# Loading the last weight matrix of a decode kernel as two tiles, with several DMAs into the second and two rows brought by sixteen 8-partition DMAs

## Chip, cores, metric

The kernel runs on one core of one Trainium2 chip. The metric is the time of one execution on the device in microseconds (us); lower is better. Engine names: PE is the matrix engine, PEld its weight loads, DVE the vector engine, ACT the scalar engine, POOL is GpSimd, SP the engine that issues nearly all DMAs (SPq is its queue of instructions).

## The reference, cut

One token of a gated mix of two blocks. Block A is attention over a long cache (4 key/value heads of 65,536 positions x 128, bf16); block B is a small MLP.

```python
q = x @ wq                                  # 1 x 4096
p = softmax(q @ k.T * Dh ** -0.5); o = p @ v # 32 query heads, 4 kv heads
a = o.reshape(1, 4096) @ wo                 # wo is 4096 x 1024 bf16: 8 MiB
b = (z1 * (w_sp * layernorm(z2) + b_sp)) @ w_out
out = g * a + (1 - g) * b
```

The caches are 134 MB (128 MiB) and everything together 162 MB, read once. The argument below is about the last 8 MiB, `wo`, seen as 32 rows of 256 KB (a row has 2 KB in each of 128 partitions).

## The kernel before

Every load takes one of five 32 KB-per-partition buffers. The output stage, with cuts (`...`):

```python
CT = 128; NKV = 5; OC = 32; D = 1024
WO_SPLIT = (16, 8, 4, 2, 1, 1)
kv = ctx.enter_context(tc.tile_pool(name="kv", bufs=NKV))

def load(src, shape, name):
    t = kv.tile([P, CT * P], BF16, name=name, tag="kv")
    ...
    nc.sync.dma_start(out=v, in_=src)          # L84: all loads are issued here
    return v
...
for j in range(NT):                            # v of the last head: four 4 MiB loads
    rest(v_units(G - 1, j, load_kv(A_v_cache, G - 1, j, "vt")))

def project(src, n, vec, c0, name, first=False, last=False):
    w = load(src, (n, D), name)
    for c in range(n):
        for j in range(NJ):                    # 8 matmuls for a row, L403
            nc.tensor.matmul(out_ps[:, j, :], lhsT=w[:, c, j * P:(j + 1) * P],
                             rhs=vec[:, c0 + c:c0 + c + 1].to_broadcast([P, W]), ...)
...
project(B_w_out..., FC, uT, 0, "wout_t", first=True)
wo_view = A_wo.rearrange("(p c) n -> p c n", c=OC)
c0 = 0
for n in WO_SPLIT:
    project(wo_view[:, c0:c0 + n, :], n, oa, c0, "wo_t", last=(c0 + n == OC))
    c0 += n
out_sb = const.tile([P, NJ], FP32, name="out_sb")
nc.vector.tensor_copy(out=out_sb[:], in_=out_ps[:, :, 0])   # first step of the epilogue
```

The framework that the kernel is written in places all semaphores. In the trace each load increments a semaphore as its data lands (the load of 16 rows 16 times, from 369.2 to 378.2 us).

## Time and profile before

| | before |
|---|---|
| time, median of 3 runs | 392.88 us (392.80 to 393.32) |
| span of the profiled run | 391.5 us |
| HBM read | 162.01 MB, 414 GB/s over the span |
| first matmul on `wo` / copy of the output out of PSUM | 378.24 / 388.66 us |

The page of the profile cuts the span into 40 slices. DMA is the busy share of the 16 DMA engines in tenths, GB/s what they moved:

```profile
DMA  8999999999999999999999999999999999999983
GB/s 329 432 434 435 437 429 433 430 430 425 430 426 430 422 424 415 410 432 434 432 429 430 422 434 432 424 425 435 427 433 434 432 423 429 427 424 428 424 352 119
```

The kernel is bound by bytes until the last two slices. There something else must be asked for: which wait ends last. The chain that ended last, in order of time (start, us, what), ends so:

```profile
344.43 33.77 DMA wo_t<-in_A_wo_dram
378.24 10.39 PE out_ps L403 x256
```

The load of the first 16 rows was issued at 344.43 and landed at 378.2. After it PE runs all 256 matmuls on `wo` without a gap. The busy times of each engine by stretch (from:to, length, busy us and count for each engine, then PE's granted clock, the DMA engines' share, GB/s) show why 256 matmuls take 10.4 us, and that DMA is already half idle at that time:

```profile
375.00:380.00 5.00, 1.76 (x34) 1.76 (x35) 0.00 (x0) 0.00 (x0) 0.00 (x0) 0.68 0.85 359
380.00:385.00 5.00, 5.00 (x116) 5.00 (x114) 0.00 (x0) 0.00 (x0) 0.00 (x0) 0.63 0.48 196
385.00:390.00 5.00, 3.90 (x118) 3.58 (x114) 0.45 (x2) 0.00 (x0) 0.00 (x0) 1.00 0.31 105
```

PE had been idle for 5.8 us before it, and starts at half clock: the granted clock was 0.50 from 376.8 to 383.7 us. Matmuls start 53 ns apart until 383.7, 31 ns apart afterwards. The idle time before a fall of the clock was not the same each time in this trace: at 376.84 PE had been idle for 4.4 us (from 372.44), at 359.77, where the granted clock also fell to half, for 2.0 us only (from 357.79).

Why is DMA half idle from 380 us on? Each load of `wo` increments its semaphore 16 times; they are read here as one increment for each of the 16 DMA engines, when its part of the load is in. The times of the 16 increments, from the semaphore records of the trace (us):

```
16 rows: 369.2 369.2 369.5 369.6 369.9 370.1 370.7 371.2 | 376.1 376.3 376.7 377.7 377.7 377.7 378.0 378.2
1 row:   378.4 378.7 378.8 379.0 379.1 379.3 379.9 380.4 | 385.5 385.8 386.8 386.8 386.8 386.9 387.1 387.3
```

So read, eight engines are about 7 us behind the other eight.

### The profile page before, as it was taken

The numbers are of one execution on the slowest core, as the hardware profiler recorded it, in microseconds if no ns is written. First come the engines' busy times: TensorE is split into PE (matmuls) and PEld (weight loads), VectorE is DVE, ScalarE is ACT, GpSimd is POOL, SyncE is SP. The second block draws the span as 40 slices with busy tenths as digits, with TensorE's granted clock in tenths as the row PEclk, the third lists the DMA queues.
The fourth block names the chain that finished last, engine by engine and source line by source line (L and its number), as shares of the span: only waits on it lengthen the run. The fifth ranks groups of instructions, "written<-read, shape, count | busy, mean of one in ns | idle before, by whom it ended". The sixth has DMA issues, their size and how long they took to land.

```text
span 391.5 us, 14960 instructions
## 1 busy us (share of the span) xinstructions
PE 301.1 (77%) x7080; PEld 291.4 (74%) x7080; DVE 152.3 (39%) x296; ACT 122.4 (31%) x139; POOL 1.0 (0%) x9
## 2 busy tenths in 40 slices
PE   0774379977889789868897878887986877887947
PEld 0774379877878779868897877877885877787836
DVE  2011036656594434435743443465443444300100
ACT  1010025544466233233453323344542323300000
POOL 1000000000000000000000000000000000000000
PEclk9999999999999989999999999999999999998979
DMA  8999999999999999999999999999999999999983
GB/s 329 432 434 435 437 429 433 430 430 425 430 426 430 422 424 415 410 432 434 432 429 430 422 434 432 424 425 435 427 433 434 432 423 429 427 424 428 424 352 119
DMA packets 6305, 162.96 MB, mean 416 GB/s; under 512 B 740, under 2 KB 740, under 8 KB 1124
## 3 DMA queue, kind: packets, MB, share of 16 engines
q1 hardware_dynamic: 6208, 162.01, 96.9%
q8 instruction: 55, 0.90, 0.8%
q14 instruction: 6, 0.05, 0.0%
q10 hardware_dynamic: 36, 0.00, 0.0%
HBM read 162.01 MB, written 0.00 MB: 414 GB/s over the span
## 4 chain that ended last, share of the span: by engine, by line
PE 62%; DMA 21%; issue 11%; ACT 3%; DVE 1%; SPq 0%; ACTq 0%
PE tps L322 30%; PE spt L301 15%; DMA kn<-in_A_k_cache_dram 12%; PE o_ps L355 12%; DMA wo_t<-in_A_wo_dram 9%; PE out_ps L403 3%; ACT scT L288 2%; PE o_ps L344 1%; ACT ktt L325 1%; ACT scT L307 1%; SPq L84 0%; PE nb_ps L279 0%; DVE mxr L264 0%; ACTq L469 0%; DVE mxr L309 0%
## 5 line engine op out<-in xcount | busy, mean ns | idle before, releaser
L322 PE MATMUL tps<-ident_b,kn 128*128 128x128 bf16 x2048 | 161.4, 222 | 23.1 <-issue 16.4
L327 DVE COPY ktt<-tps 128x1024 bf16<-128x1024 bf16 x171 | 116.6, 689 | 124.6 <-PE tps L322 124.2
L322 PEld LDWEIGHTS <-kn 128*128 128x128 bf16 x2048 | 121.7, 99 | 26.0 <-issue 19.5
L325 ACT COPY ktt<-tps 128x1024 bf16<-128x1024 bf16 x85 | 85.9, 1012 | 158.1 <-PE tps L322 158.1
L355 PE MATMUL o_ps<-scT,vt 128*128 128x64 bf16 (+1 forms) x2048 | 102.3, 198 | 17.1 <-issue 14.8
L301 PE MATMUL spt<-qT,ktt 128*128 128x64 bf16 (+7 forms) x2048 | 101.8, 192 | 15.1 <-issue 13.1
L355 PEld LDWEIGHTS <-vt 128*128 128x128 bf16 x2048 | 86.2, 99 | 20.0 <-issue 16.6
L301 PEld LDWEIGHTS <-ktt 128*128 128x128 bf16 x2048 | 84.1, 98 | 16.9 <-issue 14.3
L307 ACT CAST scT<-spt 128x512 bf16<-128x512 f32 x32 | 18.9, 589 | 24.0 <-PE spt L301 14.9
L344 PE MATMUL o_ps<-scT,ones_b 128*128 128x256 bf16 x64 | 17.7, 277 | 2.2 <-issue 1.4
L288 ACT ACTIVATE scT<-scT 128x1024 bf16<-128x1024 bf16 x16 | 16.4, 1057 | 6.2 <-DVE scT L284 6.2
L309 DVE TENSOR_TENSOR mxr<-scT,mxr 128x512 bf16<-128x512 bf16 x24 | 10.2, 425 | 15.8 <-ACT scT L307 14.3
L403 PE MATMUL out_ps<-oa,wo_t 128*128 128x64 bf16 x256 | 10.4, 212 | 5.8 <-DMA wo_t<-in_A_wo_dram 5.8
L403 PEld LDWEIGHTS <-wo_t 128*128 128x128 bf16 x256 | 10.3, 111 | 5.9 <-DMA wo_t<-in_A_wo_dram 5.9
L185 PE MATMUL z_ps<-xT,win_t 128*128 128x18 bf16 x224 | 13.7, 209 | 1.0 <-DMA win_t<-in_B_w_in_dram 0.6
L185 PEld LDWEIGHTS <-win_t 128*128 128x128 bf16 x224 | 13.7, 158 | 1.1 <-DMA win_t<-in_B_w_in_dram 0.7
L237 PE MATMUL q_ps<-xT,wq_t 128*128 128x1 bf16 x256 | 7.1, 165 | 7.5 <-DMA wq_t<-in_A_wq_dram 7.5
L237 PEld LDWEIGHTS <-wq_t 128*128 128x128 bf16 x256 | 7.0, 104 | 7.7 <-DMA wq_t<-in_A_wq_dram 7.7
L361 DVE TENSOR_TENSOR lm<-sel_q,o_ps 128x32 f32<-128x32 f32 x4 | 0.7, 183 | 30.3 <-PE o_ps L355 30.3
L284 DVE TENSOR_TENSOR scT<-scT,negm 128x1024 bf16<-128x1024 bf16 x16 | 10.7, 685 | 0.1
L344 PEld LDWEIGHTS <-ones_b 128*128 128x128 bf16 x64 | 6.3, 99 | 2.5 <-issue 1.6
L428 DVE COPY out_sb<-out_ps 128x8 f32<-128x8 f32 x1 | 0.2, 167 | 19.1 <-PE out_ps L403 19.1
(86 smaller groups left out, 41.5 us busy)
## 6 DMA issues: line engine op xcount, KB each, us to landing
kn<-in_A_k_cache_dram SPq DMA_DIRECT2D x16, 4096.0 KB, 28.2
vt<-in_A_v_cache_dram SPq DMA_DIRECT2D x16, 4096.0 KB, 26.8
wq_t<-in_A_wq_dram SPq DMA_DIRECT2D x2, 4096.0 KB, 29.7
win_t<-in_B_w_in_dram SPq DMA_DIRECT2D x2, 3584.0 KB, 15.2
wo_t<-in_A_wo_dram SPq DMA_DIRECT2D x1, 4096.0 KB, 33.8
wout_t<-in_B_w_out_dram SPq DMA_DIRECT2D x1, 3584.0 KB
wo_t<-in_A_wo_dram SPq DMA_DIRECT2D x1, 2048.0 KB
wo_t<-in_A_wo_dram SPq DMA_DIRECT2D x1, 1024.0 KB
```

Source lines behind the costliest of these rows:

```text
L185: nc.tensor.matmul(z_ps[:, hf * FC + f, :], lhsT=w[:, hf, f, :], rhs=xT[:, i * KH + c:i * KH + c + 1].to_broadcast([P, zw]), start=(i == 0 ...
L237: nc.tensor.matmul(q_ps[:, h:h + 1], lhsT=w[:, c % KH, h * DH:(h + 1) * DH], rhs=xT[:, c:c + 1], start=(c == 0 and h == 0), stop=(c == KC ...
L284: nc.vector.tensor_tensor(out=blk, in0=blk, in1=negm[:].unsqueeze(1).to_broadcast([P, CT, REP]), op=ALU.add)
L288: nc.scalar.activation(out=blk, in_=blk, func=ACT.Exp, scale=SCALE)
L301: nc.tensor.matmul(spt[g][:, o:o + n], lhsT=ktt[:, j * P:(j + 1) * P], rhs=qT[:, g * REP:g * REP + n], start=True, stop=True, skip_group_c ...
L307: nc.scalar.copy(out=blk, in_=spt[g][:].rearrange("p (c h) -> p c h", h=REP))
L322: nc.tensor.transpose(tps[:, i * P:(i + 1) * P], kn[:, u * TG + i, :], ident_b[:])
L325: nc.scalar.copy(out=ktt[:], in_=tps[:])
L327: nc.vector.tensor_copy(out=ktt[:], in_=tps[:])
L344: nc.tensor.matmul(o_ps[g][:, 2 * WL:], lhsT=ones_b[:], rhs=scT[g][:, j * CT + c:j * CT + c + SW // REP, :].rearrange("p c h -> p (c h)"), ...
L355: nc.tensor.matmul(o_ps[g][:, o0:o0 + wv], lhsT=vt[:, c, :], rhs=scT[g][:, lo:hi, :].rearrange("p c h -> p (c h)"), start=False, stop=(cg ...
L403: nc.tensor.matmul(out_ps[:, j, :], lhsT=w[:, c, j * P:(j + 1) * P], rhs=vec[:, c0 + c:c0 + c + 1].to_broadcast([P, W]), start=(first and ...
```

## The change

Intent, as the code shows it: take `wo` into two buffers in place of six, so that only the first load into each waits for a buffer, and give two rows to DMAs of 8 partitions, which run on fewer DMA engines than a DMA of 128 (in the trace of the changed kernel the first small DMA gives eight increments as its data lands, a load of 128 partitions 16).

```diff
-WO_SPLIT = (16, 8, 4, 2, 1, 1)
+WO_SPLIT = ((16,), (8, 4, 1, 1, 1, 1))
+NARROW = 2
+NB = 8
...
-    def project(src, n, vec, c0, name, first=False, last=False):
-        w = load(src, (n, D), name)
+    def project(w, n, vec, c0, first=False, last=False):
...
-    for n in WO_SPLIT:
-        project(wo_view[:, c0:c0 + n, :], n, oa, c0, "wo_t", last=(c0 + n == OC))
-        c0 += n
+    for split in WO_SPLIT:
+        t = kv.tile([P, CT * P], BF16, name="wo_t", tag="kv")
+        t = t[:].rearrange("p (c n) -> p c n", n=D)
+        b = c0
+        if split is WO_SPLIT[-1]:
+            n0 = OC - NARROW
+            for p0 in range(0, P, NB):
+                nc.sync.dma_start(out=t[p0:p0 + NB, n0 - b:, :], in_=wo_view[p0:p0 + NB, n0:, :])
+        for n in split:
+            if c0 < OC - NARROW:
+                nc.sync.dma_start(out=t[:, c0 - b:c0 - b + n, :], in_=wo_view[:, c0:c0 + n, :])
+            project(t[:, c0 - b:c0 - b + n, :], n, oa, c0, last=(c0 + n == OC))
+            c0 += n
```

The small DMAs are issued first in the second tile, before the rows 8, 4, 1, 1. In the changed kernel they have line L433, the other loads of `wo` L436, the matmuls L404.

More of the change, by code (lines that the diff above doesn't have):

```diff
@@ L62 @@
     assert DH == P and D % P == 0 and FH % P == 0 and P % H == 0
-    assert S % (P * CT) == 0 and CT % CPS == 0 and CPS % TG == 0 and sum(WO_SPLIT) == OC
+    assert S % (P * CT) == 0 and CT % CPS == 0 and CPS % TG == 0 and sum(map(sum, WO_SPLIT)) == OC
     const = ctx.enter_context(tc.tile_pool(name="const", bufs=1))
@@ L419 @@
                             op0=ALU.mult, op1=ALU.mult)
-    project(B_w_out.rearrange("(p c) n -> p c n", c=FC), FC, uT, 0, "wout_t", first=True)
+    project(load(B_w_out.rearrange("(p c) n -> p c n", c=FC), (FC, D), "wout_t"),
+            FC, uT, 0, first=True)
     wo_view = A_wo.rearrange("(p c) n -> p c n", c=OC)
     c0 = 0
-    for n in WO_SPLIT:
-        project(wo_view[:, c0:c0 + n, :], n, oa, c0, "wo_t", last=(c0 + n == OC))
-        c0 += n
+    for split in WO_SPLIT:
[11 more added lines that the diff above has]
+            c0 += n
     out_sb = const.tile([P, NJ], FP32, name="out_sb")
```

## The prediction

> **What bounds the kernel.** Bytes: 162 MB at 410-437 GB/s in nearly every slice of the page (mean 416). In the last 14 us this ends. The chain of waits closes with "DMA wo_t 33.77" (issued 344.4, landed 378.2), then 10.39 us of output matmuls without a gap: the PE window shows about 53 ns per matmul at granted clock 0.50 until 383.7, 31 ns afterwards. So the critical path ends with the landing of the 16-row tile of wo plus 256 matmuls; smaller wo loads are already there when PE reaches them. DMA is no longer full then (0.85 in 375-380 us, 0.48 in 380-385).
>
> The landing events in the trace explain this: each load of wo lands in two groups of eight engines about 7 us apart (16 rows: 369.2-371.2 and 376.1-378.2; one-row load: 378.4-380.4 and 385.5-387.3). The late eight seem to be those that also carry the 55 instruction-fetch packets (about 1 us each; estimate 55/8 x 1 us = 7 us).
>
> **What the change intends.** Two rows (512 KB) go by DMAs of 8 partitions. [...]the 8-partition output store shows eight engine increments plus one early one. If those eight are the early group, the late group loses 32 KB per engine, 1.2 us at the 1.21 us a 32 KB packet takes. The last load also loses its wait for the 16-row tile's matmuls (issued 384.7). But PE did not wait for either: 256 matmuls from 378.2 end at the same time. Expected gain by itself: about 0.
>
> **What it costs.** DMA completions rotate through eight semaphores in the trace, and the synchronizing engine waits for an old DMA on a semaphore before reusing it: the first k load, into a fresh buffer, waits on the very semaphore it reuses. Until now buffers limited the loads in flight below eight, so this was free. Now wo16 is followed at 351.6 by 16 small DMAs, then rows 8, 4, 1, 1. The 6th small one reuses the last v tile's semaphore (landed 360.0), the 7th that of w_out (368.5), the 8th that of wo16 (378.2). So SP stalls until 378.2, and the 14 ordinary rows queue behind. Engines run dry: the early group from about 372.5.
>
> Then, as estimate: nine more small issues, about 0.42 us apart (issue spacing 0.31-0.47 in the trace), 382; 1.2 us to first bytes; 14 rows at the landing spacing 4.85+2.4+0.65+0.65 = 8.55 us; last landing about 391.9. PE idles from 384.3 to about 388.2 (clock may halve), then follows the loads; its last matmul at 393.6-395 instead of 388.4. Added: 5 to 6.5 us[...].
>
> **Prediction.** 398.2 us, range 392.4 to 401.5; faster by over 2%: 0.01, within 2%: 0.83, slower by over 2%: 0.16.
>
> **What would show it.** SP's waits: DMA wo_t/wout_t/vt before small DMAs, longest about 10 us, ending 378.2. Timeline: the 8-row load issued near 382, not near 360. GB/s of the last slices: a hole near 373-383, then full rate. PE idle about 4 us between the 16-row and 8-row matmuls.
>
> **What would make it wrong.** (a) No wait on semaphore reuse within one queue: then everything is issued by 361, PE is bound as before, 392.4-393.3. (b) Partial writes of the shared tile taken as overlapping, so that each small DMA waits for the previous: 15 round trips of about 2 us, 410 us or more. (c) The small DMAs are dearer or cheaper to issue.

The sum came to 5 to 6.5 us more than before, 398.2 us as the point. Two figures of the text have these measured ones beside them: for "1.2 us to first bytes", the output store of the kernel before landed 1.2 us after its issue (389.50 to 390.70), and the first load had its first packet 1.0 us after its issue (0.74 to 1.74); for "round trips of about 2 us", the 8th small DMA of the changed kernel landed 1.9 us after its issue (378.62 to 380.51).

## More of the kernel before

The two bounds of the tail nearly coincide: the last row lands at 387.9, and PE, which never waits for it, ends its matmuls at 388.6.

## The result, and the profile after

| | before | after |
|---|---|---|
| time, median of 4 runs | 393.10 us (392.80 to 393.95) | 399.85 us (398.66 to 400.48) |
| ratio after / before | | 1.0163 (1.0138 to 1.0188) |
| span of the profiled run | 391.5 us | 398.6 us |

A ratio compares the runs of both kernels over the same rounds, so it is not quite the ratio of the medians. The change loses 1.6%, inside the range that was forecast (392.4 to 401.5) and inside "within 2%", 1.65 us above the point of 398.2.

The slices of after, beside those of before:

```profile
DMA  8999999999999999999999999999999999999464
GB/s 326 448 432 421 423 447 425 432 421 439 422 436 431 427 427 434 423 437 426 421 436 424 444 419 432 423 434 439 425 406 434 431 432 418 436 423 425 175 239 163
```

There is a hole in the third slice from the end, and then work that before had been done by then. The end of the chain of waits:

```profile
342.75 35.85 DMA wo_t<-in_A_wo_dram
381.30 1.16 SPq L433
382.51 7.14 DMA wo_t<-in_A_wo_dram
389.69 5.97 PE out_ps L404 x128
```

The 16-row load lands nearly when it did before (378.6 against 378.2). But now a second load follows it on the chain: the 8-row load goes out at 382.51, behind a small DMA (L433), and lands at 389.6. Before, it had been issued at 351.6. Busy times by stretch:

```profile
370.00:375.00 5.00, 2.28 (x74) 2.16 (x70) 0.00 (x0) 0.00 (x0) 0.00 (x0) 1.00 0.50 211
375.00:380.00 5.00, 1.35 (x26) 1.35 (x27) 0.00 (x0) 0.00 (x0) 0.00 (x0) 0.70 0.24 97
380.00:385.00 5.00, 4.95 (x107) 4.83 (x104) 0.00 (x0) 0.00 (x0) 0.00 (x0) 0.62 0.52 154
385.00:390.00 5.00, 0.31 (x6) 0.32 (x7) 0.00 (x0) 0.00 (x0) 0.00 (x0) 0.72 0.97 408
390.00:395.00 5.00, 5.00 (x111) 5.00 (x109) 0.00 (x0) 0.00 (x0) 0.00 (x0) 0.59 0.56 224
```

From 370 to 385 the DMA engines are busy 50%, 24% and 52% of the time, with 14 rows still to fetch. What SP waited for in the tail (who waited for whom: us in total, times, longest):

```profile
SPq L433 <- DMA wo_t<-in_A_wo_dram: 10.2, 1, 10.2
SPq L433 <- DMA vt<-in_A_v_cache_dram: 8.6, 1, 8.6
SPq L433 <- DMA wout_t<-in_B_w_out_dram: 8.2, 1, 8.2
```

Three issues of small DMAs waited for loads that they have no data in common with. The issue records say why. Completions rotate through eight semaphores (100 to 104 and 108 to 110), and SP waits for the earlier DMA on a semaphore before it uses that semaphore again:

```
issued at  partitions  waits for, then signals   what the semaphore carried before
342.75     128 (16 rows)             101
349.39     8                         102
349.79     8                         103
350.12     8                         104
350.45     8                         108
350.79     8           109           109         a v load, landed long before
359.70     8           110           110         the last v load
368.16     8           100           100         w_out
378.62     8           101           101         the 16 rows of wo
378.94     8           102           102         the first small DMA
...        (six more, about 0.34 us apart)
381.30     8           101           101         the 8th small DMA; this issue took 1.16 us
382.51     128 (8 rows) 102          102
382.91     128 (4 rows) 103          103
383.38     128 (1 row)  104          104
383.86     128 (1 row)  108          108
```

Before, the buffers held the number of loads in flight below eight: each load of `wo` waited for PE to free a buffer (the wait that is put down to `wo_t` here is for the last buffer, while PE itself waited for the 16 rows):

```profile
SPq L84 <- PE o_ps L355: 26.9, 4, 7.4
SPq L84 <- PE out_ps L403: 10.3, 2, 6.4
SPq L84 <- DMA wo_t<-in_A_wo_dram: 5.4, 1, 5.4
```

So the rotation cost nothing. The change took the buffer limit away and ran into this one.

PE's records show the price: before, 256 matmuls in one piece (first line); after, 128, a wait for the 8-row load, and 128 more, at half clock again:

```profile
378.24 10.38 PE L403 MATMUL out_ps<-oa,wo_t 128*128 128x64 bf16 x256 [5.80 <-DMA wo_t<-in_A_wo_dram]
378.65 6.30 PE L404 MATMUL out_ps<-oa,wo_t 128*128 128x64 bf16 x128 [6.37 <-DMA wo_t<-in_A_wo_dram]
389.69 5.96 PE L404 MATMUL out_ps<-oa,wo_t 128*128 128x64 bf16 x128 [4.74 <-DMA wo_t<-in_A_wo_dram]
```

The copy of the output starts at 395.69 instead of 388.66: 7.03 us, of which the 16-row load is 0.4.

### The profile page after: what moved, and what is told of

Its sections match the earlier page's. It is cut to its first block, busy times and chain, and to the rows that moved or that the text cites. A ratio compares the mean times of both kernels' runs of the same rounds, so it can differ in the third digit from the quotient of the medians.

```text
span 398.6 us, 14974 instructions
## 1 busy us (share of the span) xinstructions
PE 304.7 (76%) x7080; PEld 295.0 (74%) x7080; DVE 152.3 (38%) x296; ACT 122.4 (31%) x139; POOL 1.0 (0%) x9
## 4 chain that ended last, share of the span: by engine, by line
PE 52%; DMA 33%; issue 8%; ACT 2%; SPq 1%; DVE 1%; ACTq 0%
PE tps L324 26%; DMA kn<-in_A_k_cache_dram 23%; PE spt L303 13%; DMA wo_t<-in_A_wo_dram 11%; PE o_ps L357 10%; PE out_ps L404 1%; PE o_ps L346 1%; ACT ktt L327 1%; ACT scT L290 1%; SPq L433 1%; SPq L86 0%; ACT scT L309 0%; PE nb_ps L281 0%; DVE mxr L266 0%; ACTq L481 0%
## 5 line engine op out<-in xcount | busy, mean ns | idle before, releaser
L404 PE MATMUL out_ps<-oa,wo_t 128*128 128x64 bf16 x256 | 12.3, 227 | 11.1 <-DMA wo_t<-in_A_wo_dram 11.1
L404 PEld LDWEIGHTS <-wo_t 128*128 128x128 bf16 x256 | 12.0, 122 | 11.3 <-DMA wo_t<-in_A_wo_dram 11.3
L311 DVE TENSOR_TENSOR mxr<-scT,mxr 128x512 bf16<-128x512 bf16 x24 | 10.2, 425 | 16.1 <-ACT scT L309 14.5
```

## The experiments

The theory: SP is blocked because more than eight DMAs are in flight on eight semaphores; the number of DMAs counts, not their bytes. The rivals: A, sharing one tile between several DMAs costs; B, DMAs of 8 partitions, on eight engines, are slow or slow the other traffic.

Whole times are moved by up to a few us by things before the tail, so a second number is read from each trace: the *tail*, from the start of the first matmul on `wo` to the start of the copy of the output. Before it is 378.24 to 388.66, 10.42 us; after it is 378.65 to 395.69, 17.04 us.

| run | time, median | ratio to before (95%) | first matmul on wo | tail |
|---|---|---|---|---|
| before | 392.9 to 393.5 | 1 | 378.24 | 10.42 |
| after | 399.85 | 1.0163 (1.0138 to 1.0188) | 378.65 | 17.04 |
| e1_one128 | 393.33 | 1.0012 (0.9997 to 1.0027) | 378.32 | 10.71 |
| e2_nb16 | 398.82 | 1.0133 (1.0104 to 1.0162) | 380.33 | 14.30 |
| e3_rows_first | 397.50 | 1.0120 (1.0105 to 1.0136) | 378.29 | 15.40 |
| e4_pool_q | 398.59 | 1.0135 (1.0117 to 1.0153) | 383.39 | 10.33 |
| e5_spread16 | 397.82 | 1.0113 (1.0094 to 1.0131) | 381.76 | 9.87 |
| e8_tiny15 | 401.99 | 1.0215 (1.0161 to 1.0270) | 381.90 | 16.59 |
| e9_tiny5 | 396.39 | 1.0080 (1.0025 to 1.0134) | 380.02 | 10.96 |
| e10_tiny7 | 400.39 | 1.0176 (1.0126 to 1.0225) | 380.16 | 15.41 |
| e12_tiny15_xg | 399.45 | 1.0159 (1.0145 to 1.0174) | 377.98 | 17.32 |

(e6, e7 and e11 split the first tile, so their tail does not compare; they are below.)

### e1: one DMA for the two rows

```diff
-NB = 8
+NB = 128
```

> The changed kernel with the two narrow rows brought by one DMA of 128 partitions, first in the second tile (16 DMAs become 1). Theory (semaphore reuse: the 8th small DMA waits for the 16-row load, and every later load stands behind it): only six loads of wo are in flight, none waits for a load still in flight except the last one for a v tile that landed long before; time 392.4 to 393.4 us, no DMA issue of wo after 362 us. Rival A (the shared tile itself, or its partial writes, costs): stays near 398 to 400 us. Rival B (eight-engine DMAs are slow on the engines): also 392.4 to 393.4, so this run does not separate theory and B.

Measured 393.33 us. All loads of `wo` are out by 353.8; none of SP's waits in the tail is on `wo` or `w_out`. PE runs its 256 matmuls with one pause of 0.26 us:

```profile
378.32 8.25 PE L404 MATMUL out_ps<-oa,wo_t 128*128 128x64 bf16 x192 [5.94 <-DMA wo_t<-in_A_wo_dram]
386.83 2.16 PE L404 MATMUL out_ps<-oa,wo_t 128*128 128x64 bf16 x64 [0.26 <-DMA wo_t<-in_A_wo_dram]
```

Rival A is out: the shared tile and the writes into its parts cost nothing that can be measured. The two-tile arrangement alone also gains nothing.

### e2: 8 DMAs of 16 partitions

```diff
-NB = 8
+NB = 16
```

> 8 DMAs of 16 partitions each for the two rows in place of 16 of 8. Theory: the 8th still waits for the 16-row load (about 378.5), but only one small DMA is issued after it, not nine, so the 8-row load goes out at about 379.2 instead of 382.5; time about 396.5 us (395.6 to 397.5). Rival B (bytes or many small packets on only eight engines are the cost): 16 partitions spread over 16 engines, so nearly all is won back, 393 to 394 us. Rival A: 398 to 400.

Measured 398.82 us, above the expected 395.6 to 397.5, but the tail of 14.30 us says what was to be told apart: about two fifths of the loss of the tail (2.7 of 6.6 us) are back. The 8-row load was issued at 380.65, 0.3 us after the first matmul on the 16 rows, not 3.9 us after it as in the changed kernel. In the profiled run the 16-row load landed 2.1 us later than before; by 330 us the DMA records count 138.6 MB, against 139.2 before, so most of that delay (about 1.4 us, an estimate from 0.6 MB at 416 GB/s) is older than the tail. B's 393 to 394 is missed by far, though these DMAs spread over 16 engines (16 increments).

### e3: the rows before the small DMAs

```diff
-        if split is WO_SPLIT[-1]:
-            (the 16 small DMAs)
         for n in split:
+            if c0 == OC - NARROW:
+                (the 16 small DMAs)
             if c0 < OC - NARROW: ...
```

> The same 16 small DMAs on the same queue, issued after the loads of 8, 4, 1 and 1 rows instead of before them. Theory: the ordinary rows are issued at about 351, the small ones wait for semaphores one after another (4th until 378, 5th to 8th for the ordinary rows at 383 to 387, the rest for small ones), last one issued near 389.5 and landed near 391; last matmuls about 391.7; time about 396 us (394.5 to 397). Rival B: same bytes on the same eight engines, at the end of their queues: no better than the changed kernel, 399 to 400.

Measured 397.50 us, 0.5 above the range. The rows are issued by 355.5, and PE works through 240 of 256 matmuls without the stall. Then the small DMAs wait, one semaphore after another: 378.3, 383.2, 385.6, 386.2, 386.8; the last goes out at 390.4 and lands at 392.3, and PE waits 4.7 us for the last 16 matmuls. The order decides what stands behind the stall.

### e4: the small DMAs from GpSimd

```diff
-                nc.sync.dma_start(out=t[p0:p0 + NB, n0 - b:, :], ...)
+                nc.gpsimd.dma_start(out=t[p0:p0 + NB, n0 - b:, :], ...)
```

> The same 16 small DMAs in the same place, issued from GpSimd, whose completions use eight semaphores of their own. Theory: the ordinary rows are issued by 352 with no wait, the small ones wait only for one another; time 392.4 to 394 us. Rival B (eight partitions each, 4 KB per partition, is dear on the engines): 397 to 400. Rival C (SP's issue time of 16 instructions alone, 5 us): before and after would both be hidden behind 20 us of queued loads, so C predicts no loss for the changed kernel, which is already refuted unless the wait is there.

(A build of e4 gives the GpSimd DMAs the semaphores 111 to 118, eight that SP does not use.)

Measured 398.59 us: the expectation fell. The chain says where:

```profile
342.52 40.83 DMA wo_t<-in_A_wo_dram
383.39 10.31 PE out_ps L404 x256
```

The stall of SP is gone as forecast (256 matmuls in one piece, tail 10.33 us, as before the change). But the 16-row load now lands at 383.3 instead of 378.2. The small DMAs now have a queue of their own (q0, 512 packets) and land 17.1 us after their issue (median), against 40.8 us for the 16-row load; in the changed kernel the first of them, behind that load, landed 29.4 us after its issue. So they are read as running beside it instead of behind it. The DMA records show the other packets slowed: a 32 KB packet of the big loads takes 1213 ns undisturbed, on average 1274 to 1601 ns here in the stretches from 352 to 380 us. So rival B is real in this form, and the same loss came from a different cause. This run does not speak about the changed kernel; it forced the runs e5 and e7 to e12.

### e5: the same small DMAs spread over the kernel

```diff
             ku = k_units(g, j, load_kv(A_k_cache, g, j, "kn"))
+            p0 = (g * NT + j) * NB
+            nc.sync.dma_start(out=wo_n[p0:p0 + NB], in_=wo_view[p0:p0 + NB, OC - NARROW:, :])
```

(and none in the tail; `wo_n` is a tile of its own)

> The same 16 DMAs of 8 partitions from the same queue into a small tile of their own, but one after each k load, spread over the kernel, so that a semaphore comes round again only when its load has long landed; the tail has the loads of 16, 8, 4, 1, 1 rows. Theory (stall on semaphore reuse): no wait of more than a few us, 393.3 to 395.4 us (not below before, because in the changed kernel two of the eight engines of the small DMAs landed with the late group, and 64 KB more before the 16-row load puts them up to 2.4 us later). Rival B (eight-engine DMAs cost the engines dearly, wherever they are): 397 us or more, as in the GpSimd run (398.6).

Measured 397.82 us, B's side, but the run was badly designed. In the whole of it SP waited for loads in places where it had not before:

```profile
SPq L86 <- DMA kn<-in_A_k_cache_dram: 18.8, 2, 9.6
```

By 330 us 137.6 MB had come, 1.6 MB less than before: two DMAs per k load also use up the eight semaphores twice as fast. Its tail is free of a stall (9.87 us). It does not separate theory and B.

### e6: PE's backlog taken away

```diff
-WO_SPLIT = ((16,), (8, 4, 1, 1, 1, 1))
-NARROW = 2
+WO_SPLIT = ((8, 8), (8, 4, 2, 1, 1))
+NARROW = 0
```

> Two tiles, no small DMAs, loads of 8 and 8 rows into the first and 8, 4, 2, 1, 1 into the second: this takes PE's backlog away (in the kernel before, 256 matmuls run without a gap from the landing of 16 rows). If only PE's backlog bounds the tail, about 390 us. If the last bytes on the late eight engines (last landing 387.9 in the trace of before, matmuls end 388.4) bound it too, which I expect, 392.2 to 393.2, the same as before, with PE waiting for DMA near the end.

Measured 393.39 us, ratio 0.9997 (0.9984 to 1.0011). The last rows land at 388.9 in this trace and the copy of the output starts at 389.45. Taking PE's backlog away uncovers the other bound, the eight late engines. So taking away PE's backlog alone wins nothing. Relief of the late engines alone was not measured: e7, which was meant for it, slowed the other loads.

### e7 and e11: the two rows on four engines

```diff
-WO_SPLIT = ((16,), (8, 4, 1, 1, 1, 1))
+WO_SPLIT = ((8, 8), (8, 4, 1, 1, 1, 1))
-            for p0 in range(0, P, NB):
-                nc.sync.dma_start(out=t[p0:p0 + NB, n0 - b:, :], in_=wo_view[p0:p0 + NB, n0:, :])
+            for p0, p1 in ((0, 124), (124, P)):
+                nc.sync.dma_start(out=t[p0:p1, n0 - b:, :], in_=wo_view[p0:p1, n0:, :])
```

> As e6 (8 and 8 rows first), with the two narrow rows brought by two DMAs of 124 and 4 partitions in place of 16 of 8. [...]no semaphore is reused in flight, and 128 KB goes to each of four engines, 32 KB less to each other one. Four increments for each of them in the trace show whether these engines are early or late. If all four are early: last late landing about 386.7, time 391.3 to 392.2. If one or more is late: that engine ends about 3.6 us later than the others, 395 to 397.

Measured 397.07 us, ratio 1.0091 (1.0076 to 1.0106). The number of engines was as expected: the DMA of 124 partitions gave four increments by engines, at 376.0, 376.5, 376.7 and 378.9. All four come before the late group's increments for the load ahead of it (379.5 to 381.4), so all four are early engines, and the branch that I had tied to "all early" (391.3 to 392.2 us) failed. The reason is in the packets of the *other* loads: their 16 KB packets took 1099 ns on average from 370 to 375 us, against 611 ns in e1. From 370 to 375 us 245 GB/s came at a DMA share of 1.04, against 433 GB/s at 1.01 in e6. The early engines did not take work off the late ones; the other loads got slower while they tried. One premise of the expectation failed too: semaphores were reused in flight, and the last two one-row loads were issued at 359.6 and 368.0 behind the last v load and `w_out`, still before the engines had reached them.

e11 is e7 with another source. Its output is wrong, which doesn't matter for the time.

```diff
-in_=wo_view[p0:p1, n0:, :]
+in_=(4 KB pieces that lie one after another in A_k_cache)
```

> e7 again (two DMAs of 124 and 4 partitions on four engines), but they read 4 KB pieces that follow one another in the k cache in place of rows 64 KB apart: the result is wrong on purpose. In e7 packets of 16 KB of the other loads took about 1.1 us in place of 0.61 us while these DMAs ran. If the 64 KB step of the source is the cause: packets back at 0.61 us, 392.5 to 394 us. If it is which engine writes to which partitions: still 1.1 us, 396 to 397.5 us.

Measured 396.85 us; 16 KB packets 1078 ns in the same stretch. The 64 KB step of the source is not the cause. What is left is the destination or the engines; which of them, and how, was not shown. e1 and e2 bear on it: both bring the two rows over all 16 engines (16 increments), in 128 packets of 4 KB, e1 as one DMA of 128 partitions and e2 as eight of 16. From 370 to 375 us the 32 KB packets took 1228 ns in e1 and 1417 ns in e2. So few engines are not needed for the slowing. Whether it comes from which engine serves which partitions stays open: e2 also has more DMAs, and no run varied the destination alone.

### e8, e9, e10: DMAs without bytes

e1, which is as fast as before, with 15, 5 or 7 DMAs of 2 bytes after the two-row DMA:

```diff
+            tiny = const.tile([1, 16], BF16, name="tiny")
+            for i in range(15):     # 5, 7
+                nc.sync.dma_start(out=tiny[:, i:i + 1], in_=A_x[0, 0:1, i:i + 1])
```

> The fast kernel of e1 (one DMA of 128 partitions brings both narrow rows) with 15 more DMAs behind it, of 2 bytes each into a scratch tile: 16 DMAs before the ordinary rows as in the changed kernel, but no bytes on eight engines. Theory (number of DMAs against eight semaphores): the 7th small one waits for the 16-row load, later ones for one another, the 8-row load is issued at about 383, 398.5 to 400 us like the changed kernel. Rival B (small DMAs on few engines slow the other packets): stays at 393 to 394.

> The same with 5 DMAs of 2 bytes. Theory: the 8-row load waits for w_out only (368.5, while both groups of engines still have work); the 4-row load waits for the 16-row load (378.3), when the late engines still have 8 rows to fetch; nearly free: 392.8 to 394.2 us.

> The same with 7 DMAs of 2 bytes. Theory: the last of them waits for the 16-row load and the 8-row load for the narrow rows behind it (late engines 379.5): issued at 379.6, about 3 us before that of e8; 395 to 397 us. A step between 5 and 7, not a slope of a few tenths of a us per DMA.

Measured 401.99, 396.39 and 400.39 us, each about 2 us or more above its range. The tails behave as the theory has it: with 5 DMAs of 2 bytes 10.96 us, and within it PE never waits over 0.72 us for a load; with 7, 15.41 us; with 15, 16.59 us. It is a step and not a slope: two more DMAs of 2 bytes cost 4.45 us, eight further ones 1.2 us. With 5 the 8-row load waits only for `w_out` and goes out at 370.3; with 7 it waits behind the 16-row load and goes out at 381.4. PE with 5 (first three lines) and with 7:

```profile
380.02 5.46 PE L404 MATMUL out_ps<-oa,wo_t 128*128 128x64 bf16 x128 [4.96 <-DMA wo_t<-in_A_wo_dram]
386.20 2.16 PE L404 MATMUL out_ps<-oa,wo_t 128*128 128x64 bf16 x64 [0.72 <-DMA wo_t<-in_A_wo_dram]
388.68 2.26 PE L404 MATMUL out_ps<-oa,wo_t 128*128 128x64 bf16 x64 [0.32 <-DMA wo_t<-in_A_wo_dram]
380.16 5.53 PE L404 MATMUL out_ps<-oa,wo_t 128*128 128x64 bf16 x128 [5.82 <-DMA wo_t<-in_A_wo_dram]
389.95 5.59 PE L404 MATMUL out_ps<-oa,wo_t 128*128 128x64 bf16 x128 [4.26 <-DMA wo_t<-in_A_wo_dram]
```

The surplus in the whole times lies before the tail: the first matmul on `wo` comes at 380.0 to 381.9. By 330 us these runs had received 137.7 to 138.7 MB, e1 139.6 MB, though up to there their instructions are the same. One difference was left: the scratch tile of 32 bytes had moved all big tiles up by 32 bytes (the first of them from byte 26,880 of its partitions to 26,912, as a build of the kernels shows). The packets bear its mark: the median 32 KB packet takes 1216 ns in e8 to e10 and 1213 ns in every other run, and the 55 instruction fetches take 1046 to 1066 ns on average, against 970 in e11, which ran on the same chip without the move.

### e12: the same without the scratch tile

```diff
-                nc.sync.dma_start(out=tiny[:, i:i + 1], in_=A_x[0, 0:1, i:i + 1])
+                nc.sync.dma_start(out=xg8[0:1, 0, i:i + 1], in_=A_x[0, 0:1, i:i + 1])
```

> e8 again, but the 15 DMAs of 2 bytes rewrite the same values of x in a tile that exists already, so that no scratch tile is allocated and the big tiles keep the addresses of e1 (the scratch tile of e8 to e10 had moved them all by 32 bytes, and there the 16-row load landed 2 to 4 us later than in the kernel before). Theory: tail as in e8, 16.5 us from the landing of the 16-row load to the last output matmul; if the shift of the tiles caused the earlier delay, that landing is back at 378 to 379 us and the time is 398.6 to 400.2 us, that of the changed kernel; if the 2-byte DMAs themselves caused it, landing 380 to 382 and 401 to 403 us. Rival B (bytes on eight engines are the loss): 393 to 394.

Measured 399.45 us, ratio 1.0159 (1.0145 to 1.0174); the changed kernel has 1.0163. The 16-row load lands early again (first matmul 377.98). How much the move of the tiles had cost is not settled: e8 and e12 ran on different chips, their intervals of the ratio overlap (1.0161 to 1.0270, 1.0145 to 1.0174), and in e2, whose tiles were not moved, the 16-row load landed 2.1 us late as well. SP's waits (first three lines) and the chain of waits (last two) have the form of the changed kernel's:

```profile
SPq L435 <- DMA wo_t<-in_A_wo_dram: 10.4, 2, 9.4
SPq L435 <- DMA wout_t<-in_B_w_out_dram: 8.2, 1, 8.2
SPq L435 <- DMA vt<-in_A_v_cache_dram: 6.5, 1, 6.5
381.50 7.25 DMA wo_t<-in_A_wo_dram
388.80 6.48 PE out_ps L404 x128
```

So e1 plus 15 DMAs that carry 30 bytes in all loses what the changed kernel loses. Rival B, which asks for 393 to 394, is not needed to explain the changed kernel. Its own cost is real (e4, e7), but small in the changed kernel: nine of the 16 small DMAs are issued after the 16 rows have landed (from 378.62 us), when no other load is in flight. The first seven do run beside the 16-row load, whose packets take 1321 ns on average from 365 to 370 us in place of 1213; it lands 0.4 us later than before.

## Why the prediction was right

The stated range (392.4 to 401.5) also holds the time of the kernel before, 393.1, so a time inside it says little. What makes the prediction right is the chain of waits that it named:

- **The stall on semaphore reuse: right.** Forecast: the 6th, 7th and 8th small DMA wait for the last v load (360.0), `w_out` (368.5) and the 16 rows (378.2), the longest wait about 10 us. Measured: 359.7, 368.2, 378.6, longest 10.2 us. e12 shows that it is sufficient, e1 that without it nothing is lost, e9 and e10 where the limit lies.
- **The 8-row load near 382: right**, 382.5.
- **The hole and the drain: right in kind, too small in size.** Forecast 1.2 + 4.85 = 6.05 us from issue to landing of the 8 rows; the chain shows 7.14. In e12 it is 7.25 with no bytes on eight engines, so the small DMAs are not the reason. The start was close to the forecast (first packet at 383.5, 1.0 us after the issue). The term that was too small is the 4.85: it is the landing spacing of a full queue, and this load starts on idle engines. Its 16 KB packets that start before 385 us take 873 ns on average, against 611 ns in e1's full queue. The last landing was 393.4, forecast 391.9.
- **PE's end: slightly outside.** Forecast last matmul at 393.6 to 395, measured end 395.65. PE idled 4.74 us (forecast about 4), and its clock did halve, as was put as a possibility: 0.59 granted from 390 to 395 us. Therefore PE did not just follow the loads: its last 128 matmuls took 5.97 us without a gap and ended 2.2 us after the last landing. At 31 ns each they would have taken about 4 us (an estimate), so about 2 us of the 7.03 are the slow clock.
- **Extra semaphore waits of PE: not seen.** The last 128 matmuls stand as one piece of 5.96 us in the timeline.
- **"If those eight are the early group": wrong in part.** Increments of the first small DMA: 368.7, 368.9, 369.0, 369.1, 369.8, 370.9, and 376.8, 378.8. Six are early, two late. It did not matter for the time, because the drain was set by the ordinary rows.
- **Expected gain of the intent about 0: supported.** e1 and e6 stand at 1.0012 and 0.9997, and moving rows to engines that were all early (e7) lost 0.9%. Relief of the late engines without that side effect was not measured.
- That the late eight are those that fetch instructions was an estimate (from 55 packets, 948 ns each on average in the trace of the kernel before) and stays one; no run tested it.

What stays open: by what path DMAs of other than 128 partitions slow the packets of the others, and why and by how much moving the tiles by 32 bytes costs time (e12 and e8 differ in that, in where 30 bytes go, and in the chip they ran on; nothing finer was tried). No run beat the kernel before.

## What to carry to other kernels

Count the DMAs in flight, not only their bytes: here, with completions on eight rotating semaphores, the ninth DMA waited for the first (10.2 us), and every load behind it in SP's program waited too (the 8-row load went out at 382.51 us instead of 351.6), so put the big loads ahead of small ones and keep the number low. Before shifting work to idle units, look for what else bounds the same moment (here a PE backlog and the late DMA engines ended within 1 us of each other), and check that the busy ones do not slow down when their neighbours change pattern (16 KB packets took 1099 ns in e7, 611 in e1). When an experiment needs a scratch tile, put it where it moves no other tile, or write into one that is there (first matmul on `wo` at 381.90 us with the move in e8, at 377.98 without it in e12, on another chip).
